# Softmax row sums without a stop in DRAM, and a plan that knows the DMA queue's limit, in a fused attention + mixer kernel

## The chip, the cores and the metric

The kernel runs on one core of a Trainium2 chip. TensorE (PE) multiplies matrices, ScalarE (ACT), VectorE (DVE) and GpSimd (POOL) do element-wise work, and SyncE (SP) issues nearly all DMAs, in the order in which they stand in its program. The metric is device time in microseconds (us) of one execution; lower is better.

## The reference

One token block of 2048 tokens x 512 features goes through two branches that share the input; a per-token gate mixes them.

```
g = sigmoid((x * gate_w).sum(-1))
a = attention(x)     # 32 heads of 16; q,k,v = x @ wqkv; softmax(q k^T / 4) v; then @ wo
h = gelu(layernorm(x) @ w1)          # four feature groups, shifted by +1,-1,+2,-2 tokens
x1 = x + shift(h) @ w2
b = x1 + gelu(layernorm(x1) @ w3) @ w4      # inner width 1792
out = g * a + (1 - g) * b
```

## The kernel before

**The work.** Attention scores are computed transposed, in tiles of 128 keys x 512 queries of one head: 2048 tiles in all. They come in 32 rounds of 64 tiles. A round is a chunk `c` of 512 queries, a group `G` of eight heads and a parity `p`, so it has four heads; four heads sit in the four 32-row groups of the PE array. A PE matmul (line L1536) puts one tile's scores into one of eight PSUM banks. Then the exponential is taken in one of two ways:

- ACT takes two or three banks in one `Exp` activation (L1631) and writes bf16 probabilities.
- DVE computes an approximation from the bits of the number (L1663), one bank at a time, and three shifted copies of a pair of tiles are made by DVE (L1706) and POOL (L1708); the four copies are added up by four PE matmuls instead of one.

The matmul with V (L1761) adds a tile into the round's accumulator bank. V has a column of ones, so row 0 of each head's 32-row group is the softmax row sum.

**The end of a round** (`finish_round`). DVE copies the accumulator to SBUF (`accsb`, L1782). The four row sums (4 x 512 floats) are spread over 128 partitions so that DVE can invert them quickly: one DMA stores them in DRAM (`den`, L1784), a second loads them as 128 x 16 (`pk`, L1786). DVE takes the reciprocal (L1789) and multiplies by the gate (L1790). A DMA stores the factors in DRAM (`rr`, L1792), four DMAs broadcast one row each to 32 partitions of `bcs` (L1796), POOL multiplies (`oT`, L1800), and four DMAs move each head's 16 rows to their place in `oD` (L1804), the operand of the output projection. `oD` of a pair of rounds (p = 0 and 1) belongs together. Other DMAs go through the same queue of SP: weights, the transposed loads of x (`DMA_TRANSPOSE`), and the layer norm's rows that POOL makes (`xn`, L1358), SP stores (`xn_dram`, L1362) and loads back transposed (L1368).

**The order.** Nothing is scheduled on the chip by itself: the kernel runs a model of the engines while it is built (`Sim`) and writes down instructions in the order in which the model started them. Each job has planned durations: `dma(lat, ..., hold)` is an SP job that holds the queue for `hold` ns and lands `lat` ns after its start. A table `STEPS` sets some 40 parameters of the planner's rules (priorities, how far ahead to work, how many tiles DVE may take) for each eighth of a round, 256 stages in all. On the chip every engine then runs its list in order, and waits where an operand is late. `start()` writes the first loads by hand with planned issue times, and `first()` writes the first transposes (L1206), projections (L1198) and copies by hand.

Of the kernel before, what the change touches and what calls it, by code (L numbers as in the profile page):

```python
# [11 lines left out]
ALU = mybir.AluOpType  # L12
BF16 = mybir.dt.bfloat16
F32 = mybir.dt.float32
# [177 lines left out]
class Sim:  # L192
# [6 lines left out]
    def __init__(self, slots):  # L199
# [24 lines left out]
        self.readers = {}  # L224
        self.usable = [0.0] * 8
# [108 lines left out]
    def try_engine(self, e):  # L334
# [136 lines left out]
def kernel(  # L471
# [77 lines left out]
        0: dict(P1_PRIO=0.312, GP2=0.15, DVE_STOP=8, DVE_STOP_L=12, DVE_ALONE=138, SL0=-150, SL1=130, IDLE_NS=864,  # L549
            BRES=2, AHEAD=16, PV_FULL=0.947, PV_IDLE=0.25, PRESS=22, ROT=1, AT_SH=118, HOLE=3, CAP3=5, LIMD=4, GATE=4,  # L550
            AFIRST=1, LIMA=2, JOIN=1),
        1: dict(P1_PRIO=0.743, S_PRIO=0.178, DVE_STOP_L=7, URG=2, DVE_ALONE=-158, SL0=45, SL1=0, PV_IDLE=0.731,
            E_PRIO=0.25, JOIN=2),
        2: dict(ROT=3, E_PRIO=2, ROWM=7),
        3: dict(P1_PRIO=0.414, S_PRIO=0.625, GP2=0.8, DVE_STOP_L=16, URG=3, DVE_ALONE=2, SL0=0, B_LOW=5, DVE_WAIT=2,
            AHEAD=24, AHEAD2=32, PV_IDLE=0.5, MAXU=3, DUE_SH=-6, AT_SH=69, MAXG=2, CAP3=0, LIMD=3, GATE=3, E_PRIO=0.25,
            AGE=6000, ROWM=3, JOIN=0),
        4: dict(GP2=1, EARLY=64, SL1=-150),
        5: dict(P1_PRIO=0.743, S_PRIO=0.3, DVE_STOP=2, DVE_STOP_L=7, URG_L=18, DVE_ALONE=362, SL1=60, B_LOW=8, BRES=4,
            AHEAD2=24, PV_FULL=0.916, PV_IDLE=0.25, PRESS=18, MAXU=2, ROT=2, HOLE=7, MAXG=1, CAP2=5, CAP3=7, AFIRST=2,  # L560
            AGE=9000, ROWM=99, LIMA=3),
        6: dict(P1_PRIO=0.312, S_PRIO=0.214, DVE_STOP=13, DVE_STOP_L=16, URG_L=12, DVE_ALONE=2, B_LOW=3, BRES=0,
            DVE_WAIT=1, AHEAD2=32, PV_FULL=1, PV_IDLE=0.117, ROT=0, DUE_SH=-14, HOLE=0, MAXG=3, GATE=4, AFIRST=1,
            AGE=3000, JOIN=1),
        7: dict(S_PRIO=0.38, E_PRIO=2, AGE=12000),
        8: dict(S_PRIO=0.214, DVE_STOP_L=7, URG=2, EARLY=99, IDLE_NS=537, B_LOW=0, BRES=4, AHEAD=3, AHEAD2=16,
            PV_IDLE=0.25, MAXU=4, ROT=2, DUE_SH=-6, E_PRIO=0.25, AFIRST=2, AGE=9000, LIMA=4, JOIN=0),
        9: dict(P1_PRIO=0.414, S_PRIO=0.3, DVE_STOP=6, DVE_STOP_L=16, URG=3, URG_L=18, DVE_ALONE=-81, SL0=130, SL1=130,
            IDLE_NS=459, B_LOW=5, BRES=2, DVE_WAIT=3, AHEAD=24, AHEAD2=32, PV_FULL=0.916, PV_IDLE=0.731, PRESS=22,
            MAXU=9, DUE_SH=-9, AT_SH=34, HOLE=3, MAXG=1, CAP2=6, CAP3=0, LIMD=4, GATE=3, E_PRIO=2, AGE=3000, LIMA=3,  # L570
            JOIN=1),
        10: dict(B_LOW=8, PRESS=26, MAXU=2, AFIRST=1, AGE=9000, ROWM=1),
        11: dict(AT_SH=69, ROWM=5),
        12: dict(S_PRIO=0.625, GP3=0.9, DVE_STOP=13, DVE_ALONE=-158, SL0=45, SL1=60, IDLE_NS=374, PV_FULL=0.86,
            PV_IDLE=0.25, MAXU=3, ROT=3, AT_SH=0, HOLE=2, CAP3=7, LIMD=3, AFIRST=2, AGE=20000, ROWM=0, JOIN=0),
        14: dict(MAXU=2),
        15: dict(DVE_WAIT=1, E_PRIO=0.1, AFIRST=1),
        16: dict(GP3=0.633, AHEAD2=24, HOLE=0, MAXG=3, LIMD=4, AFIRST=2, AGE=3000),
        17: dict(DVE_ALONE=362),
        18: dict(P1_PRIO=0.2, S_PRIO=0.5, GP2=0.3, GP3=0.967, DVE_STOP=8, URG_L=12, DVE_ALONE=-158, EARLY=64, SL0=130,  # L580
            SL1=45, DVE_WAIT=2, AHEAD=9, AHEAD2=32, PV_FULL=0.947, MAXU=7, ROT=2, AT_SH=34, HOLE=2, MAXG=1, CAP3=6,
            AFIRST=0),
        19: dict(MAXU=3),
        20: dict(DVE_WAIT=4, AHEAD=12, MAXG=2, AGE=6000),
        21: dict(CAP3=4, GATE=2, ROWM=1),
        22: dict(GP2=0.8, URG_L=18, DUE_SH=0),
        23: dict(GP2=0.15, DVE_WAIT=2, PV_IDLE=0.117),
        24: dict(P1_PRIO=0.136, S_PRIO=0.38, GP2=1, GP3=0.8, URG=11, DVE_ALONE=500, EARLY=99, SL0=0, SL1=0, IDLE_NS=864,
            B_LOW=0, BRES=0, DVE_WAIT=3, AHEAD=5, PV_FULL=0.97, MAXU=4, ROT=3, DUE_SH=32, HOLE=7, CAP3=0, GATE=3,
            E_PRIO=2, AFIRST=2, AGE=12000, ROWM=99, ACC2=2),  # L590
        25: dict(GP3=0.5, DVE_STOP=6, URG=2, DVE_ALONE=138, AHEAD=24, PV_IDLE=0.25, ROT=0, DUE_SH=-14, HOLE=2, CAP3=5,
            AGE=20000, ACC2=1),
        26: dict(GP2=0.15, URG=8, AHEAD=16, PV_FULL=0.813, CAP3=4, ACC2=2),
        27: dict(SL1=60, ACC2=1),
        28: dict(GP2=1, GP3=0.967, URG_L=12, DVE_ALONE=-81, SL1=0, PV_FULL=0.916, ACC2=2),
        29: dict(GP3=0.5, SL0=130, SL1=45, ROT=1, E_PRIO=0.1, LIMA=2),
        30: dict(DVE_STOP=2),
# [1578 lines left out]
```

## Time and profile before

| | |
|---|---|
| median of 3 runs | 731.88 us (731.85 to 732.23) |
| the profiled execution's own time | 731.34 us |
| its span, from first to last instruction | 729.4 us |
| ACT busy | 713.2 us (98%) |
| PE busy | 719.9 us (99%) |
| DVE busy | 698.0 us (96%) |
| POOL busy | 481.0 us (66%) |
| DMA | 38.27 MB in 69543 packets, mean 52 GB/s |

A matmul that was issued into a full pipeline counts as busy until its modelled end, so PE's share does not show whether PE had time to spare; the waits do. A group's "busy" is the union of its instructions in time, its mean is that of single instructions, which overlap at their ends. The profiled execution ran 0.54 us under the median of the timed runs.

### The profile page before, as it was taken

Reading aid. Unit: us, or ns where it says so; the run is one execution under the profiler, and the core shown is the slowest. Engines: PE = TensorE matmul, PEld = TensorE weight load, DVE = VectorE, ACT = ScalarE, POOL = GpSimd, SP = SyncE. Lnnn points to the kernel's source line nnn. Section 1 sums busy time; section 2 is a strip of 40 time slices with the busy share of each in tenths; the row PEclk is TensorE's granted clock in tenths of the full one; section 3 lists DMA queues with packets and bytes.
Section 4 is the critical chain, followed back from the end, with each engine's and each line's share of the span. In section 5 each row is a group of like instructions: output and inputs, shape, how many; then the busy total and the mean of one; then the engine's idle time right before and its main releaser. Section 6 shows DMA issues by size and latency. Waiting matters only on the chain.

```text
span 729.4 us, 23745 instructions
## 1 busy us (share of the span) xinstructions
PE 719.9 (99%) x9533; PEld 214.3 (29%) x9533; DVE 698.0 (96%) x1461; ACT 713.2 (98%) x728; POOL 481.0 (66%) x502
## 2 busy tenths in 40 slices
PE   9999999999999999999999999999999999999997
PEld 5334322232332222223222222222222232222222
DVE  6999899999999999999999999999999999999997
ACT  6999989999999999999999999999999999999995
POOL 2786767778786876685556556686777856564451
PEclk9999999999999999999999999999999999999999
DMA  9222422323123210141111101221100131000001
GB/s 188 79 61 54 101 71 46 65 50 89 61 67 79 59 41 22 45 137 53 24 26 35 28 22 29 63 80 28 41 19 21 36 102 26 25 28 21 18 19 40
DMA packets 69543, 38.27 MB, mean 52 GB/s; under 512 B 46893, under 2 KB 64317, under 8 KB 69433
## 3 DMA queue, kind: packets, MB, share of 16 engines
q1 hardware_dynamic: 68472, 36.23, 19.7%
q8 instruction: 74, 1.21, 0.7%
q10 hardware_dynamic: 960, 0.52, 0.3%
q14 instruction: 37, 0.29, 0.2%
HBM read 21.07 MB, written 6.81 MB: 38 GB/s over the span
## 4 chain that ended last, share of the span: by engine, by line
PE 80%; ACT 13%; DVE 2%; issue 2%; DMA 1%; POOL 1%; SPq 0%; ACTq 0%; DVEq 0%
PE banks L1761 29%; PE banks L1536 26%; PE banks L1134 24%; ACT prob L1631 12%; ACT hT L1378 1%; DVE prob L1706 1%; DMA wq<-in_A_wqkv_dram 1%; DMA xn_dram<-xn 1%; DVE prob L1663 0%; PE banks L2111 0%; POOL prob L1708 0%; ACT L1378 0%; DVE hB L1431 0%; PE banks L1291 0%; PE banks L1198 0%
## 5 line engine op out<-in xcount | busy, mean ns | idle before, releaser
L1631 ACT ACTIVATE prob<-banks 128x1024 bf16<-128x1024 f32 (+1 forms) x705 | 669.1, 1121 | 3.1 <-PE banks L1536 2.8
L1708 POOL TENSOR_SCALAR prob<-prob 128x1024 uint16<-128x1024 uint16 x364 | 374.5, 1047 | 180.7 <-DVE prob L1706 118.5
L1663 DVE TENSOR_SCALAR prob<-banks 128x512 uint16<-128x512 f32 (+1 forms) x577 | 385.0, 693 | 12.7 <-PE banks L1536 8.0
L1761 PE MATMUL banks<-prob,V 128*17 128x512 bf16 (+1 forms) x3818 | 319.6, 381 | 2.1 <-POOL prob L1708 1.5
L1536 PE MATMUL banks<-q,kT 32*128 32x512 bf16 x2048 | 275.7, 384 | 1.4 <-ACT prob L1631 0.2
L1706 DVE TENSOR_SCALAR prob<-prob 128x1024 uint16<-128x1024 uint16 x521 | 192.3, 423 | 3.6 <-POOL prob L1708 2.3
L1536 PEld LDWEIGHTS <-kT 32*128 32x128 bf16 x2048 | 69.1, 90 | 289.0 <-ACT prob L1631 265.5
L1761 PEld LDWEIGHTS <-V 128*17 128x17 bf16 (+1 forms) x3818 | 73.5, 88 | 120.0 <-issue 96.4
L1134 PE MATMUL banks<-xnT,w 128*32 128x512 bf16 x1152 | 92.1, 383 | 0.0
L1800 POOL TENSOR_TENSOR oT<-accsb,bcs 128x512 bf16<-128x512 f32 x31 | 39.5, 1275 | 28.8 <-DVE prob L1706 24.8
L1134 PE MATMUL banks<-w,hT 128*32 128x512 bf16 x696 | 57.6, 383 | 0.0
L1134 PEld LDWEIGHTS <-w 128*32 128x32 bf16 x1904 | 40.3, 95 | 48.3 <-issue 28.1
L1134 PE MATMUL banks<-w,w 128*32 128x256 bf16 (+1 forms) x752 | 38.0, 309 | 0.0
L1134 PE MATMUL banks<-w,hB 128*32 128x512 bf16 x448 | 37.7, 382 | 0.0
L1358 POOL TENSOR_SCALAR xn<-x_sb,rs,nm 128x512 bf16<-128x512 bf16 x32 | 25.0, 785 | 13.8 <-DVE prob L1706 3.7
L1145 PE MATMUL banks<-w,oD 32*128 32x512 bf16 x56 | 21.5, 384 | 0.0
L1338 DVE BATCH_NORM_STATS2 st<-x_sb 128x6 f32<-128x512 bf16 x32 | 21.4, 680 | 0.0
L1782 DVE COPY accsb<-banks 128x512 f32<-128x512 f32 x31 | 21.1, 680 | 0.1
L1134 PE MATMUL banks<-w,oD 128*32 128x512 bf16 x184 | 21.0, 384 | 0.1
L1134 PEld LDWEIGHTS <-hT 128*32 128x32 bf16 x696 | 14.9, 95 | 19.9 <-issue 14.0
L1134 PE MATMUL banks<-w,wq 128*32 128x512 bf16 x240 | 19.8, 383 | 0.0
L1378 ACT ACTIVATE hT<-hT 128x7168 bf16<-128x7168 bf16 (+1 forms) x3 | 19.4, 6452 | 0.0
(100 smaller groups left out, 273.6 us busy)
## 6 DMA issues: line engine op xcount, KB each, us to landing
bcs<-rr SPq DMA_DIRECT2D x124, 64.0 KB
xn_dram<-xn SPq DMA_DIRECT2D x32, 128.0 KB
w<-in_B_w_dram SPq DMA_DIRECT2D x8, 512.0 KB
w<-in_B_w_dram SPq DMA_DIRECT2D x8, 448.0 KB
oD<-oT SPq DMA_DIRECT2D x124, 16.0 KB
x_sb<-in_A_x_dram SPq DMA_DIRECT2D x3, 512.0 KB
out_dram<-ot SPq DMA_DIRECT2D x12, 128.0 KB
w<-in_A_wqkv_dram SPq DMA_DIRECT2D x2, 256.0 KB
```

The source lines that it names most:

```text
L1134: units.append([Op("col", j, lambda j=j, lf=lf, rf=rf, n0=n0, n1=n1, st=st, sp=sp: nc.tensor.matmul(get()[32 * j:32 * j + 32, n0:n1], lhsT ...
L1145: o = Op("row", i, lambda: nc.tensor.matmul(get(), lhsT=lf(0, P)[rows], rhs=rf()[rows], start=False, stop=True, tile_position=(32 * i, 0), ...
L1338: a = dve(600, deps, lambda: nc.vector.bn_stats(out=sb.slot[:], in_=x_sb[:, t, :]), prio=6, at=at, acq=[sb])
L1358: g = gp(750, [m], lambda t=t, xb=xb: nc.gpsimd.tensor_scalar(out=xb.slot[:], in0=x_sb[:, t, :], scalar1=rs[which][:, t:t + 1], scalar2=nm ...
L1378: g = nc.scalar.activation(out=ap, in_=ap, func=ACT.Gelu_apprx_tanh)
L1536: o = Op("row", i, lambda: nc.tensor.matmul(dst(), lhsT=kT[G][32 * i:32 * i + 32, kt * P:(kt + 1) * P], rhs=qbuf[G, c].slot[32 * i:32 * i ...
L1631: job = act(hold, ops, lambda: nc.scalar.activation(out=prob[:, pb.cut(), :].bitcast(BF16), in_=unit()[:, rb.cut(), :], func=ACT.Exp, scal ...
L1663: return nc.vector.tensor_scalar(out=prob[:, b0.cut() if w == 2 else b0.bufs[h0].slot, :], in0=unit()[:, rb.cut() if w == 2 else rb.bufs[0 ...
L1706: return nc.vector.tensor_scalar(out=cut(k), in0=cut(0), scalar1=float(SHIFT * k), scalar2=None, op0=ALU.add)
L1708: return nc.gpsimd.tensor_scalar(out=cut(k), in0=cut(0 if both else 2), scalar1=1.0, scalar2=float(SHIFT * (k if both else 1)), op0=ALU.mu ...
L1761: return nc.tensor.matmul(one(accs[r])[32 * i:32 * i + n, :], lhsT=lhs(n), rhs=rhs(), start=st and not edge, stop=True, tile_position=(0, ...
L1800: n = gp(1250, d3, lambda: nc.gpsimd.tensor_tensor(out=ob.slot[:], in0=ab.slot[:], in1=bb.slot[:], op=ALU.mult), acq=[ob], frees=[ab, bb], ...
```

## The change

In the order in which they act:

- **Start.** The load of the second chunk of x (512 KB) is made to wait for an earlier DMA, the third load of x rows; what stands behind it on SP waits with it. One of nine warm-up matmuls is dropped. Of the five copies of transposed x, ACT makes one and DVE four (before: two and three). The planned times of this piece are rewritten.
- **End of a round.** The row sums go from `accsb` to `pk` in one DMA within SBUF; `den` is gone. One DMA broadcasts all four rows of `rr`. For the first 30 rounds the whole of `oT` is stored in DRAM (`o_dram`) in one DMA, and once both rounds of a pair are there one DMA loads that pair's `oD`. Round 30 keeps the four direct DMAs; round 31 has none, as before.
- **Plan.** The model lets SP start a DMA only when the one eight places earlier has landed by its own reckoning (`sent`). Four small loads for the last chunk's gate (`zL`) are put off to tile 300 and later. The whole table `STEPS` has other values (245 entries, before 244), so the order of all engines is another one.

The 2048 tiles are split between the engines almost as before: ACT's program had 657 activations of two banks and 48 of three, and now has 661 and 45, which is one tile less for ACT and one more for DVE. In the rounds SP's program loses 31 `den` DMAs, 93 of 124 `bcs` and 120 of 124 `oD<-oT`, and gains 30 stores and 15 loads through `o_dram`: 199 DMAs less.

```diff
+        self.sent = [0.0] * 8
...
             end = max(end, self.queue + 1500.0)
+            land = max(self.t + 0.65 * (j.hold + j.lat), min(end, self.queue + 1500.0))
+            self.sent = self.sent[1:] + [land]
+            if self.sent[0] > self.t_free[e]:
+                self.t_free[e] = self.sent[0]
+                self.push(self.t_free[e], None)
...
     STEPS = {
-        0: dict(P1_PRIO=0.312, GP2=0.15, DVE_STOP=8, DVE_STOP_L=12, DVE_ALONE=138, SL0=-150, SL1=130, IDLE_NS=864,
+        0: dict(P1_PRIO=0.312, GP2=0.15, DVE_STOP=8, DVE_STOP_L=12, URG=8, DVE_ALONE=138, SL0=-75, SL1=130, IDLE_NS=864,
...
+    o_dram = dpool.tile([4 * NCH, 4, 2, 32, 512], BF16, name="o_dram")
...
+    def behind(inst, first):
+        tc.add_manual_dep(inst.ins, first.ins.name, mybir.DependencyInfo(
+            mybir.DependencyClass.Sync, mybir.DependencyReason.DATA), reason="load order")
...
-    j_x1 = [start("SP", 4900.0, lambda q: q.dma_start(out=x_sb[:, 4:8, :], in_=x_src(1, 0, 4)))]
+    issue["SP"] = 4500.0
+    j_x1 = [start("SP", 2900.0, lambda q: q.dma_start(out=x_sb[:, 4:8, :], in_=x_src(1, 0, 4)))]
+    behind(insts[-1], insts[2])
...
-        for _ in range(9):
+        for _ in range(8):
...
-                cp = nc.scalar.copy if i in (1, 3) else nc.vector.tensor_copy
+                cp = nc.scalar.copy if i == 2 else nc.vector.tensor_copy
...
-                in_=zE_dram[S - 512:S].rearrange("(b e) -> e b", e=32)), prio=6)
+                in_=zE_dram[S - 512:S].rearrange("(b e) -> e b", e=32)), prio=6).at = 300 + 20 * j
...
-            j_att[c].append(d)
+        for G in range(4 if c < NCH - 1 else 3):
+            j_att[c].append(dma(3300.0, [att_done[c * 8 + 2 * G], att_done[c * 8 + 2 * G + 1]], lambda c=c, G=G: nc.sync.dma_start(
+                out=oDbuf[c, G].slot[:], in_=o_dram[4 * c + G].rearrange("j p q n -> (j p) q n")[:, 1:DH + 1, :]),
+                acq=[oDbuf[c, G]], prio=1))
...
-        d0 = dma(2000.0, [e], lambda: nc.sync.dma_start(out=db.slot[:], in_=ab.slot[0:P:32, :]), prio=1, acq=[db],
-                 frees=[ab], hold=580.0)
-        d1 = dma(2800.0, [d0], lambda: nc.sync.dma_start(
-            out=kb.slot[:], in_=db.slot[:].rearrange("j (b e) -> (j b) e", e=16)), prio=1, acq=[kb], frees=[db],
-            hold=400.0)
+        d1 = dma(3000.0, [e], lambda: nc.sync.dma_start(out=kb.slot[:], in_=ab.slot[0:P:32, :]), prio=1, acq=[kb],
+                 frees=[ab], hold=450.0)
...
-        for j in range(4):
-            d3.append(dma(3000.0, [d2], lambda j=j: nc.sync.dma_start(
-                out=bb.slot[32 * j:32 * j + 32, :], in_=rb.slot[j, :].partition_broadcast(32)),
-                acq=[] if j else [bb], frees=[rb], prio=1))
-            d3[j].need = bb if j else None
...
+        d3 = dma(3400.0, [d2], lambda: nc.sync.dma_start(
+            out=bb.slot[:], in_=rb.slot[:].unsqueeze(1).broadcast_to([4, 32, 512])), acq=[bb], frees=[rb], prio=1)
...
+        if r < NR - 2:
+            dma(3200.0, [n], lambda: nc.sync.dma_start(out=o_dram[4 * c + G, :, p, :, :], in_=ob.slot[:]), frees=[ob, fin], prio=1,
+                hold=400.0)
+            return
```

Two places show how the order moves. The first is DVE at the very start, from the copies of the transposed first chunk (`w`) to the first query block (`q`); before:

```order
L1211 COPY w_97<-banks 128x2x256 x2
L1211 COPY w_97<-banks 128x256
L1216 CAST kT_64<-banks 128x256
L1218 TENSOR_SCALAR q_107<-banks,mE 128x256
L1224 TENSOR_SCALAR q_107<-banks,mO 128x256 x2
```

and now:

```order
L1224 COPY w_98<-banks 128x2x256 x2
L1224 COPY w_98<-banks 128x256 x2
L1229 CAST kT_64<-banks 128x256
L1231 TENSOR_SCALAR q_108<-banks,mE 128x256
L1237 TENSOR_SCALAR q_108<-banks,mO 128x256 x2
```

One more quarter-size copy stands on DVE, and the sequence behind it is the same.

The second is SP from the first broadcast of a round's factors to the row sums of round 2. `bcs`, `rr`, `oT`, `oD`, `den` and `pk` are the buffers of the round's end told above, `xnT` is the transposed load of the normalised x, `w<-in_B_w` a weight load; before:

```order
L1796 DMA bcs_113<-rr_134 32x512 x4
L1368 DMA_TRANSPOSE xnT_104<-xn_dram 128x512 x4
L1796 DMA bcs_113<-rr_135 32x512 x4
L1804 DMA oD_116<-oT_114 16x512 x4
L1082 DMA w_102<-in_B_w_dram 128x4x512
L1362 DMA xn_dram<-xn_105 128x512
L1362 DMA xn_dram<-xn_106 128x512
L1804 DMA oD_116<-oT_115 16x512 x4
L1784 DMA den_133<-accsb_111 4x512
L1362 DMA xn_dram<-xn_105 128x512
L1786 DMA pk_130<-den_133 128x16
```

and now:

```order
L1381 DMA_TRANSPOSE xnT_105<-xn_dram 128x512 x2
L1807 DMA bcs_114<-rr_132 128x1x512
L1375 DMA xn_dram<-xn_106 128x512
L1375 DMA xn_dram<-xn_107 128x512
L1807 DMA bcs_114<-rr_133 128x1x512
L1813 DMA o_dram<-oT_115 4x32x512
L1095 DMA w_103<-in_B_w_dram 128x4x512
L1375 DMA xn_dram<-xn_106 128x512
L1375 DMA xn_dram<-xn_107 128x512
L1800 DMA pk_131<-accsb_112 128x1x16
```

From the first broadcast to the landing of round 2's row sums SP issued 26 DMAs, and now issues 9. Four transposed loads stood between the two rounds' broadcasts; two of them now stand ahead of the first broadcast and two ahead of those shown.

More of the change, by code (lines that the diff above doesn't have):

```diff
@@ L973 @@
         "pk": slots("pk", 3, [P, 16], F32),
-        "den": slots("den", 3, [4, 512], F32, dpool),
         "rr": slots("rr", 3, [4, 512], F32, dpool),
@@ L1228, in first @@
         sim.emit(t, mm)
[L1229 to L1231 removed]
+        sim.t_free["PE"], sim.arr, sim.mode = t + 3440.0, [t + 3520.0] * 4, "full"
+        sim.push(t + 3440.0, None)
+        at_time(t + 2200.0, bt[1:])
         for k in range(KT):
[L1233 to L1236 removed]
+            j_xT[0, 0, k] = at_time(t + 2200.0)
+        j_q[0, 0, 0] = at_time(t + 3550.0)
+        j_ka.append(at_time(t + 3070.0, [ba, wb["x00"], wb["x00"], wb["k"]]))
+        j_k[0, 0] = act(275, [at_time(t + 3520.0)], lambda: nc.scalar.copy(out=kT[0][:, 256:512], in_=one(bb)[:, 0:256]),
                         prio=0, frees=[bb])
@@ L1452, in mlp2_down @@
                     lambda G=G: W("o")[:, G, :]) for G in range(ng)]
-            wdeps = [dl_w["o"]] + j_att[c][:2 * ng]
+            wdeps = [dl_w["o"]] + j_att[c][:ng]
             last = c == NCH - 1
@@ L1833 @@
             PLAN["w4", 4 * c + t] = int(a + (b - a) * t / 4)
-    first(3450.0)
+    first(3480.0)
     begun = [j_ka[0], j_q[0, 0, 0]]
```

730 lines of the change are left out of this document (360 added, 370 removed).

## The prediction

> **What bounds the kernel now.** I read the page's busy times first, then ACT's groups by shape, then the waits, then the timeline where ACT starts, stops and stalls.
>
> ```profile
> PE 719.9 (99%) x9533; PEld 214.3 (29%) x9533; DVE 698.0 (96%) x1461; ACT 713.2 (98%) x728; POOL 481.0 (66%) x502
> L1631 ACT ACTIVATE prob<-banks 128x1024 bf16<-128x1024 f32 (+1 forms) x705 | 669.1, 1121 | 3.1 <-PE banks L1536 2.8
> ...
> L1631 ACT ACTIVATE prob<-banks 128x1024 bf16<-128x1024 f32 x657 | 614.0, 1089 | 2.9 <-PE banks L1536 2.7
> L1631 ACT ACTIVATE prob<-banks 128x1536 bf16<-128x1536 f32 x48 | 74.0, 1550 | 0.2 <-PE banks L1536 0.2
> ...
> PEld L1536 <- ACT prob L1631: 265.5, 640, 0.6
> ```
>
> Three engines look full. The wait row decides: the score matmuls' weight loads waited 640 times, 265.5 us in all, for ACT to give banks back, while ACT's exponentials sat idle 3.1 us for anything. So ACT is the bound and PE follows it. The three places where ACT does not stream are its start, its end and one stretch between:
>
> ```profile
> 8.78 5.97 ACT L1631 ACTIVATE prob<-banks 128x1536 bf16<-128x1536 f32 x5 [0.17 <-PE banks L1536]
> ...
> 333.35 11.99 ACT L1631 ACTIVATE prob<-banks 128x1024 bf16<-128x1024 f32 x13
> ...
> 713.07 7.47 ACT L1631 ACTIVATE prob<-banks 128x1024 bf16<-128x1024 f32 x8
> ...
> 721.50 0.72 DVE L2122 STREAM_TRANSPOSE accsb<-banks 128x512 f32<-128x512 f32 x1 [1.60 <-PE banks L1761]
> ```
>
> The first exponential starts at 8.78, the last ends at 713.07 + 7.47 = 720.54, and the tail to 729.4 is 8.9 us. A quiet stretch has 13 two-bank exponentials in 11.99 us; the last takes some 1.09 to its end (the mean of one in the row of 657), so one comes every (11.99 - 1.09) / 12 = 0.908 us. By the same 0.18 us of overlap a three-bank one takes 1.550 - 0.18 = 1.37. Then the 705 need 657 x 0.908 + 48 x 1.37 = 662.3 us, and they held ACT for 669.1 + 3.1 = 672.2. So between start and tail at most 9.9 us can be had without taking work off ACT.
>
> **The start.** The chain of waits and the timeline:
>
> ```profile
> 1.68 4.56 DMA wq<-in_A_wqkv_dram
> ```
> ```profile
> 1.12 3.06 PE L1113 MATMUL banks<-zero 128*128 128x384 bf16 x9 [1.12 <-DVE zero L1102]
> ...
> 2.17 0.58 SPq L1053 DMA_DIRECT2D x_sb<-in_A_x_dram  x1
> ...
> 3.97 1.91 PE L1206 MATMUL banks<-idb,x_sb 128*128 128x128 bf16 x16
> ...
> 5.07 1.01 ACT L1211 COPY w<-banks 128x512 bf16<-128x512 bf16 x2 [1.44 <-PE banks L1206]
> ...
> 6.28 0.61 PE L1198 MATMUL banks<-w,wq 128*128 128x256 bf16 x4 [0.39 <-DMA wq<-in_A_wqkv_dram]
> ...
> 9.13 1.07 PE L1165 MATMUL banks<-idb,x_sb 128*128 128x128 bf16 x16
> ```
>
> The first projection waited for `wq`, on its way for 4.56 us, while the 512 KB of the second chunk, issued at 2.17, shared the DMA engines. The transposes were done at 3.97 + 1.91 = 5.88. Holding the big load takes that wait: -0.39 us. A warm-up matmul is a ninth of 3.06 us, so dropping one lets the transposes start up to 0.34 earlier, if x is there; the copies that the first projection needs then end on DVE instead of on ACT, and no later. Together -0.73. Against it: the transposes took 1.91 us for 16, and the same 16 at 9.13 took 1.07, so the array was still slow until about 5.6, and projections that begin sooner may run slow. Four at 6.28 took 0.61; at half speed they take some 0.4 more. The range is 0 to -0.8, and I take **-0.7**, as only the first projections can still fall into the slow time. What the hold costs: SP itself stands until x rows are there, about when the transposes begin (3.97), so the second chunk (2.17 before), the V weights and eight transposed loads behind them are issued about 2 us later. The transposes at 9.13 cover that if the load then lands in about 4 us from its issue; if it is 0.6 late, ACT's third exponential is, and the gain sinks to the lower end.
>
> The Trainium skill's page "TensorE: Matmul & The Clock Gate", in Part 1, says that the array runs at half speed until about 3.4 us of sustained work have been seen. By that rule alone the array, at work from 1.12, would have been fast from some 4.5 us on, and the start would gain the full 0.73 (an estimate by that page); the two transpose rows put the change later, and the measurement decides.
>
> **The stretch from 72 to 100 us.** The groups of that window, then what SP, POOL, DVE and ACT did in it:
>
> ```profile
> L1631 ACT ACTIVATE prob<-banks 128x1024 bf16<-128x1024 f32 (+1 forms) x28 | 26.9, 1101 | 2.4 <-PE banks L1536 2.4
> ```
> ```profile
> 69.41 1.72 SPq L1796 DMA_DIRECT2D bcs<-rr  x4
> 76.97 2.58 SPq L1796 DMA_DIRECT2D bcs<-rr  x4
> 79.59 3.13 SPq L1804 DMA_DIRECT2D oD<-oT  x4
> 84.47 2.41 SPq L1804 DMA_DIRECT2D oD<-oT  x4
> 86.98 0.54 SPq L1784 DMA_DIRECT2D den<-accsb  x1
> ```
> ```profile
> 72.83 1.28 POOL L1800 TENSOR_TENSOR oT<-accsb,bcs 128x512 bf16<-128x512 f32 x1 [1.69 <-DMA bcs<-rr]
> 82.20 1.27 POOL L1800 TENSOR_TENSOR oT<-accsb,bcs 128x512 bf16<-128x512 f32 x1 [2.37 <-DMA bcs<-rr]
> 87.66 2.02 POOL L1358 TENSOR_SCALAR xn<-x_sb,rs,nm 128x512 bf16<-128x512 bf16 x2 [1.15 <-DMA xn_dram<-xn]
> ```
> ```profile
> 90.73 0.43 DVE L1706 TENSOR_SCALAR prob<-prob 128x1024 uint16<-128x1024 uint16 x1 [2.29 <-POOL prob L1708]
> 91.97 0.25 DVE L1789 RECIPROCAL pk<-pk 128x16 f32<-128x16 f32 x1 [0.81 <-DMA pk<-den]
> ```
> ```profile
> 92.36 1.02 ACT L1631 ACTIVATE prob<-banks 128x1024 bf16<-128x1024 f32 x1 [1.14 <-PE banks L1536]
> 94.27 1.02 ACT L1631 ACTIVATE prob<-banks 128x1024 bf16<-128x1024 f32 x1 [0.89 <-PE banks L1536]
> 95.67 2.99 ACT L1631 ACTIVATE prob<-banks 128x1024 bf16<-128x1024 f32 x3 [0.37 <-PE banks L1536]
> ```
>
> This is one causal chain. SP was issuing broadcasts and head moves without a break from 76.97 to 86.88, and three stores and loads behind them came late. POOL stood 1.69 + 2.37 + 1.15 = 5.2 us for DMAs, DVE 2.29 for POOL and 0.81 for the row sums, and ACT lost 1.14 + 0.89 + 0.37 = 2.4 us for scores that PE could not issue. The price is a little more, since the overlap is lost too: from 92.36 to 94.27 and to 95.67 are steps of 1.91 and 1.40, and the one before 92.36 began some 1.02 + 1.14 earlier; three steps took 5.47 us instead of 3 x 0.908, which is 2.75 more. It is nearly all of the idle time that ACT's exponentials show for scores (2.4 of 2.8 us in the run). The new SP order has 9 DMAs in that place instead of 26, and the plan now counts the queue's depth, so it no longer puts POOL's and DVE's work where its data can't be. The ends are 0 (the jam moves elsewhere) and -2.8 (all of it goes); I take **-2.8**, since three separate causes in the chain, the four broadcasts, the head moves and the `den` hop, shrink at once.
>
> **The quiet rounds.** The round's DMAs late in the run:
>
> ```profile
> 698.48 2.43 SPq L1804 DMA_DIRECT2D oD<-oT  x4
> 701.80 0.53 SPq L1784 DMA_DIRECT2D den<-accsb  x1
> 703.50 0.34 SPq L1786 DMA_DIRECT2D pk<-den  x1
> ...
> 709.04 1.72 SPq L1796 DMA_DIRECT2D bcs<-rr  x4
> 715.55 2.42 SPq L1804 DMA_DIRECT2D oD<-oT  x4
> ```
> ```profile
> 704.93 1.21 PE L1134 MATMUL banks<-w,oD 128*32 128x512 bf16 x12
> ```
>
> Per round SP's issue time falls by the `den` DMA's 0.53, three quarters of 1.72 and most of 2.42, some 3.5 us; a hop of 703.50 - 701.80 = 1.7 us goes, and a store plus a load take the place of the direct moves, one landing more, bounded by that same hop: 1.7 to 3 us. None of it is on ACT's path: `oD` of the last pair but one was issued at 698.48 and first used at 704.93, and the other pairs have hundreds of microseconds. So **0**, and at most 1 us late at 704.93, where PE would stand with two or three banks of scores issued ahead.
>
> **ACT's own work.** Four two-bank exponentials more and three three-bank ones less: 4 x 0.908 - 3 x 1.37 = **-0.5**. The tail code is the same: 0.
>
> **The sum.** -0.7 - 2.8 - 0.5 = -4.0 on a profiled time of 731.34: 727.3. The median lies 0.54 above the profiled execution (731.88), so I forecast **727.9**. The rest of the new table reorders everything but takes nothing else off ACT; I cost it at 0, with the 9.9 us above as the bound of a gain, and the rivals below for a loss.
>
> **The rivals.**
>
> *The small gaps go too.* A plan that knows the queue may also lift part of the other 9.9 - 2.8 = 7.1 us of short stalls. Half of them gives 727.9 - 3.5 = 724.4, all of them 720.8. For it: all 256 stages are set anew. Against it: those gaps come from PE and banks and not from DMAs, as DVE's waits for DMAs are the 0.8 us above and POOL's are the rows above. 0.22.
>
> *The jam only moves.* Two rounds' ends pile up there because the gate's result comes late, and that is unchanged. If the stall comes back a little later in the same size, what is left is -0.5 and a start gain of 0.3: 731.1. 0.09.
>
> *The one broadcast is slow* (the other side). Its destination is 128 partitions, but its source has four rows, and one DMA of 4 x 64 KB could run on four of the 16 DMA engines.
>
> ```profile
> q1 hardware_dynamic: 68472, 36.23, 19.7%
> ...
> bcs<-rr SPq DMA_DIRECT2D x124, 64.0 KB
> ```
>
> 36.23 MB took 19.7% of 16 x 729.4 engine-us, 63 engine-us per MB, so 256 KB take 16.6: 1.0 us on 16 engines, 4.2 on four. Before, `bcs` landed 72.83 - 69.41 = 3.4 us after the first of four issues, 2.0 after the last; the plan now counts 3.4 in all. On four engines the landing comes at 2.0 - 1.0 + 4.2 = 5.2, 1.8 us behind the plan, in each of 31 rounds. In the jam 5.2 us of POOL's waits cost ACT 2.4, about 0.46 for one. If every round's lateness met a POOL that was ready, 31 x 1.8 x 0.46 = 26 us would be lost; the plan's slack decides, and from 9 us of POOL waits on (a sixth of that) the gain of 4.0 is used up. With a third of it the time is 727.9 + 8.6 = 736.5. Against it: only the two `oT` of the jam waited for `bcs` at all, the other 29 came after its landing anyway (in the last round 715.55, where the moves begin, less 1.28 is 5.2 us after 709.04), and 63 engine-us per MB is an average over small packets, while these are 2 KB each. 0.12.
>
> The Trainium skill's page "DMA: Bandwidth & Descriptors", in "Why a DMA increments its semaphore by 16 and not by 1", says that the number of engines is the largest up to 16 that divides the outermost sizes of both sides. For 4 and 128 that is four, which speaks against this edit; the former pieces, 32 rows each, got 16. No run here shows it yet.
>
> **How the numbers follow.** The forecast has 0.57: 725.5 to 730.4. About 0.2% (1.5 us) is what a measurement of this kernel can tell from no change, so "same" is 730.4 to 733.3. Faster: 0.57 + 0.22 = 0.79; same: the moved jam, 0.09; slower: 0.12. The range reaches down to 722.5, between half and all of the small gaps, and up to 732.5, over the moved jam and a slow broadcast that just eats the gain.
>
> **What would show it.** Right: the first exponential at 8.0 or sooner and no `wq` wait over 0.2; no idle of ACT over 0.5 between 72 and 100; SP never at work for 10 us without a break there; POOL's waits for `bcs` still few. Wrong: the second chunk's transposes waiting for x at 8 to 9 us; DVE's reciprocal waiting for the row sums; POOL waiting for `bcs` in round after round and PE behind it; a stall of ACT of over 2 us at another place.

## The result, and the profile after

The changed kernel took **736.73 us** at the median (736.26 to 737.13, four runs), the kernel before 731.87 (731.83 to 732.23, four runs on the same chip): a ratio of 1.0065, with a 95% interval of 1.0048 to 1.0082. It is slower by 4.9 us. The forecast was 727.9, faster by 4.0, with a range up to 732.5; the sign was wrong and the time lies outside. The third rival, *the one broadcast is slow*, had been worked out at 736.5. Two runs of the experiments below, at 917.1 and 834.8 us with granted clocks of 0.66 and 0.75, lay far outside all others and are left out of every figure.

The busy times, the exponentials and POOL's product with the factors on the page of the changed kernel (the code has moved by some lines: 1631 is now 1647, 1706 is 1722, 1800 is 1809):

```profile
span 734.7 us, 23442 instructions
PE 721.3 (98%) x9558; PEld 216.3 (29%) x9559; DVE 708.2 (96%) x1456; ACT 715.7 (97%) x728; POOL 487.3 (66%) x507
L1647 ACT ACTIVATE prob<-banks 128x1024 bf16<-128x1024 f32 (+1 forms) x706 | 671.9, 1099 | 6.2 <-PE banks L1552 4.6
L1809 POOL TENSOR_TENSOR oT<-accsb,bcs 128x512 bf16<-128x512 f32 x31 | 41.0, 1324 | 34.5 <-DMA bcs<-rr 19.2
bcs<-rr SPq DMA_DIRECT2D x31, 256.0 KB
```

The exponentials' own idle has doubled, from 3.1 to 6.2 us, and 4.6 of that is for scores. DVE is busy for 10.2 us more (708.2 against 698.0) with five instructions fewer. And POOL's product stood idle for 34.5 us before its 31 instances, 19.2 of them for the broadcast (before: 28.8 us, 4.1 of them for the broadcast). POOL's row in the waits of the changed kernel (us in total, times, longest):

```profile
POOL oT L1809 <- DMA bcs<-rr: 19.2, 14, 4.3
```

Before there were two such waits, the 1.69 and 2.37 of the jam that the prediction quotes. Now there are 14 among 31 rounds. The chain of waits of the changed kernel (start, us, what) has the broadcast on it as well, early and late:

```profile
1.68 4.09 DMA wq<-in_A_wqkv_dram
70.57 5.67 DMA bcs<-rr
79.42 7.60 DMA xn_dram<-xn
...
603.26 4.95 DMA bcs<-rr
```

The start came as forecast in direction, with the first exponential at 8.32 instead of 8.78. The first projections still stood 0.24 us for `wq`, and the second chunk's transposes (8.66) did not wait for their held load. The timeline of the changed kernel (start, us, engine, line, the idle before in brackets):

```profile
5.81 0.61 PE L1211 MATMUL banks<-w,wq 128*128 128x256 bf16 x4 [0.24 <-DMA wq<-in_A_wqkv_dram]
8.66 1.07 PE L1178 MATMUL banks<-idb,x_sb 128*128 128x128 bf16 x16
8.32 5.97 ACT L1647 ACTIVATE prob<-banks 128x1536 bf16<-128x1536 f32 x5 [0.17 <-PE banks L1552]
```

The jam did not go. In the timeline of the changed kernel it stands at 82 to 91 us, SP's issues first, then POOL, then ACT:

```profile
70.57 0.58 SPq L1807 DMA_DIRECT2D bcs<-rr  x1
77.62 0.55 SPq L1807 DMA_DIRECT2D bcs<-rr  x1
76.31 1.28 POOL L1809 TENSOR_TENSOR oT<-accsb,bcs 128x512 bf16<-128x512 f32 x1 [1.59 <-DMA bcs<-rr]
84.53 1.27 POOL L1809 TENSOR_TENSOR oT<-accsb,bcs 128x512 bf16<-128x512 f32 x1 [4.26 <-DMA bcs<-rr]
87.18 1.52 POOL L1371 TENSOR_SCALAR xn<-x_sb,rs,nm 128x512 bf16<-128x512 bf16 x2 [1.38 <-DMA xn_dram<-xn]
81.79 5.83 ACT L1647 ACTIVATE prob<-banks 128x1024 bf16<-128x1024 f32 x6 [0.77 <-PE banks L1552]
87.84 1.02 ACT L1647 ACTIVATE prob<-banks 128x1024 bf16<-128x1024 f32 x1 [0.22 <-PE banks L1552]
90.76 5.61 ACT L1647 ACTIVATE prob<-banks 128x1024 bf16<-128x1024 f32 x6 [1.90 <-PE banks L1552]
```

ACT's group for the stretch from 72 to 100 us, which the prediction shows for the kernel before (28 exponentials, 2.4 us idle), is now:

```profile
L1647 ACT ACTIVATE prob<-banks 128x1024 bf16<-128x1024 f32 x28 | 26.3, 1077 | 3.0 <-PE banks L1552 2.9
```

SP's issue time did shrink as forecast (0.58 for a broadcast instead of 1.72 or 2.58), but POOL waited for broadcasts as before, 1.59 and 4.26 us, and ACT lost 0.77 + 0.22 + 1.90 = 2.89 us. These two products began 76.31 - 70.57 = 5.74 and 84.53 - 77.62 = 6.91 us after the issue of their broadcast, where the plan has 3.4. ACT's loss over the whole run can be counted from the starts of all the exponentials: a two-bank one takes 0.904 us to the next start where nothing stalls, a three-bank one 1.331. With that and ACT's other work taken off, ACT stalled for 19.7 us between its first and last exponential, against 13.4 before: 6.3 more. With 0.46 gained at the start, 0.4 at ACT's own work and 0.2 in the tail that makes 5.2; the profiled executions differ by 734.7 - 729.4 = 5.3.

How long one broadcast takes shows in the DMA view of each kernel from the issue of the last round's broadcast on (each figure is the rate over 0.12 us); first the kernel after:

```profile
GB/s 0 0 0 0 0 0 0 0 0 0 0 51 51 51 51 34 119 85 119 85 119 85 119 85 102 102 102 102 102 102 102 102 102 51 51 188 34 17 0 0
```

Nothing moves for 1.3 us, and then 256 KB move at about 100 GB/s; the packets of 2 KB ran from 715.38 to 718.60, 3.22 us, so the data was there 4.6 us after the issue at 714.05 and POOL's product began after 5.04. In no round of this kernel did the product begin sooner than 4.86 us after the broadcast's issue. The plan counts 3.4. A stretch within another round's broadcast, in the table by stretches (us, busy and instructions of PE, PEld, DVE, ACT and POOL, granted clock, DMA share, GB/s):

```profile
699.20:702.00 2.80, 2.80 (x39) 0.77 (x35) 2.69 (x6) 2.80 (x4) 2.40 (x3) 1.00 0.23 91
```

A DMA share of 0.23 is 3.7 of 16 engines, so I read it as the broadcast from four rows running on four. This agrees with the rule that the prediction cites from the Trainium skill's page "DMA: Bandwidth & Descriptors", section "Why a DMA increments its semaphore by 16 and not by 1".

### The profile page after: what moved, and what is told of

It is laid out like the page before. It is cut to its first block, busy times and chain, and to the rows that moved or that the text cites. A ratio compares the mean times of both kernels' runs of the same rounds, so it can differ in the third digit from the quotient of the medians.

```text
span 734.7 us, 23442 instructions
## 1 busy us (share of the span) xinstructions
PE 721.3 (98%) x9558; PEld 216.3 (29%) x9559; DVE 708.2 (96%) x1456; ACT 715.7 (97%) x728; POOL 487.3 (66%) x507
## 4 chain that ended last, share of the span: by engine, by line
PE 80%; ACT 7%; DVE 6%; DMA 3%; issue 2%; POOL 1%; SPq 0%; DVEq 0%; POOLq 0%; ACTq 0%
PE banks L1777 29%; PE banks L1552 27%; PE banks L1147 23%; ACT prob L1647 5%; DVE prob L1722 3%; DVE prob L1679 2%; DMA bcs<-rr 1%; DMA xn_dram<-xn 1%; ACT hB L1391 1%; POOL prob L1724 1%; DMA wq<-in_A_wqkv_dram 1%; PE banks L2120 0%; POOL xn L1371 0%; PE banks L2098 0%; DVE accsb L1798 0%
## 5 line engine op out<-in xcount | busy, mean ns | idle before, releaser
L1724 POOL TENSOR_SCALAR prob<-prob 128x1024 uint16<-128x1024 uint16 x369 | 378.7, 1046 | 171.6 <-DVE prob L1722 113.1
L1722 DVE TENSOR_SCALAR prob<-prob 128x1024 uint16<-128x1024 uint16 x519 | 201.1, 443 | 1.4 <-PE banks L1777 0.9
L1777 PEld LDWEIGHTS <-V 128*17 128x17 bf16 (+1 forms) x3821 | 75.1, 88 | 121.3 <-issue 94.8
L1809 POOL TENSOR_TENSOR oT<-accsb,bcs 128x512 bf16<-128x512 f32 x31 | 41.0, 1324 | 34.5 <-DMA bcs<-rr 19.2
L1147 PE MATMUL banks<-w,hT 128*32 128x512 bf16 x692 | 62.0, 383 | 0.2 <-DVE accsb L1798 0.2
L1444 DVE CAST hB<-banks 128x512 bf16<-128x512 f32 x28 | 18.8, 675 | 0.2 <-PE banks L1147 0.2
```

The lines of the kernel that those rows point to most:

```text
L1147: units.append([Op("col", j, lambda j=j, lf=lf, rf=rf, n0=n0, n1=n1, st=st, sp=sp: nc.tensor.matmul(get()[32 * j:32 * j + 32, n0:n1], lhsT ...
L1722: return nc.vector.tensor_scalar(out=cut(k), in0=cut(0), scalar1=float(SHIFT * k), scalar2=None, op0=ALU.add)
L1724: return nc.gpsimd.tensor_scalar(out=cut(k), in0=cut(0 if both else 2), scalar1=1.0, scalar2=float(SHIFT * (k if both else 1)), op0=ALU.mu ...
L1777: return nc.tensor.matmul(one(accs[r])[32 * i:32 * i + n, :], lhsT=lhs(n), rhs=rhs(), start=st and not edge, stop=True, tile_position=(0, ...
L1809: n = gp(1250, [d3], lambda: nc.gpsimd.tensor_tensor(out=ob.slot[:], in0=ab.slot[:], in1=bb.slot[:], op=ALU.mult), acq=[ob], frees=[ab, bb ...
```

## The experiments

The theory after this result (A): the landing of the one broadcast, 1.2 us behind the plan by its data and some 1.5 by the product's start, costs the kernel what the rest of the change gains. Rivals: the new order itself is worse (B), or the row sums' or heads' new path is (C). Ratios are against the kernel before, run beside each experiment on the same chip; its medians there were 731.95 to 732.39.

### Four broadcasts in the place of the one

Everything is as in the changed kernel, its order too; only the broadcast is four DMAs again.

```diff
-        d3 = dma(3400.0, [d2], lambda: nc.sync.dma_start(
-            out=bb.slot[:], in_=rb.slot[:].unsqueeze(1).broadcast_to([4, 32, 512])), acq=[bb], ...
+        d3 = dma(3400.0, [d2], lambda: [nc.sync.dma_start(
+            out=bb.slot[32 * j:32 * j + 32, :], in_=rb.slot[j, :].partition_broadcast(32)) for j in range(4)][-1],
```

> The changed kernel with every engine's order as it is, but the broadcast of a round's factors is issued as four DMAs of 32 partitions each, one behind the other at the place of the one. Theory A (the one broadcast lands about 5.0 us after its issue, since few DMA engines carry it, where the plan counts 3.4): oT follows 3.4 to 4.5 us after the first issue, POOL's waits for bcs fall from 19.2 us to under 5, ACT's losses between exponentials fall by 4 to 7 us, time 730 to 732.5. Theory B (the new order itself stalls ACT, whatever the broadcast does): POOL's waits fall too, but the time stays at 735 to 737.5.

Measured: **727.9 us** (727.56 to 728.59, six runs), ratio 0.9946 (0.9928 to 0.9964). That is 8.8 us below the changed kernel, and the forecast's own number; it is also below the 730 that theory A had allowed, so the late landing cost more than expected. The span, the groups of the page, and POOL's wait in this kernel:

```profile
span 725.6 us, 23598 instructions
L1647 ACT ACTIVATE prob<-banks 128x1024 bf16<-128x1024 f32 (+1 forms) x706 | 668.4, 1113 | 1.2 <-PE banks L1552 0.7 <-POOL prob L1724 0.4
POOL oT L1810 <- DMA bcs<-rr: 1.3, 1, 1.3
```
```profile
L1647 ACT ACTIVATE prob<-banks 128x1024 bf16<-128x1024 f32 x31 | 28.7, 1105 | 0.4 <-POOL prob L1724 0.4
```

The exponentials' idle is 1.2 us instead of 6.2, POOL waits once for `bcs`, and in the stretch from 72 to 100 us (the second fence, its groups) there are 31 exponentials with 0.4 us idle, where the kernel before had 28 with 2.4 and the changed kernel 28 with 3.0. The last round's broadcast in this kernel's DMA view, from its first issue:

```profile
GB/s 0 0 0 0 0 0 0 34 85 85 171 120 273 137 154 103 137 137 137 154 154 205 69 34 0 0 0 0 0 0 0 0 0 0 0 0 137 68 0 0
```

The first of the four starts while SP is still issuing the others, and the data is there 2.9 us after the first issue instead of 4.6. Theory A is borne out, and B and C fall as causes of the loss: the new order and the other edits are all in this kernel.

### The one broadcast in the kernel before

```diff
-            d3.append(dma(3000.0, [d2], lambda j=j: nc.sync.dma_start(
-                out=bb.slot[32 * j:32 * j + 32, :], in_=rb.slot[j, :].partition_broadcast(32)),
+            d3.append(dma(3000.0, [d2], lambda j=j: None if j else nc.sync.dma_start(
+                out=bb.slot[:], in_=rb.slot[:].unsqueeze(1).broadcast_to([4, 32, 512])),
```

> The kernel before with every engine's order as it is, but its four broadcast DMAs are one, at the place of the first. Theory A: the landing moves from 3.4 to about 5.0 us after the first issue; in the former order oT stood 4.2 to 5.9 us after it, so only some rounds wait: POOL's waits for bcs grow from 4.1 to 8 to 16 us and the time rises by 1 to 4 us, to 733 to 736. Theory B: the broadcast is harmless, time 731.3 to 732.5.

Measured: 733.43 us (731.79 to 735.25, ten runs), ratio 1.0016 (1.0001 to 1.0031): some 1.2 us slower, not 8.8. POOL's wait:

```profile
POOL oT L1800 <- DMA bcs<-rr: 7.8, 7, 3.6
```

Seven waits and 7.8 us, where the kernel before has two and 4.1, cost 1.2. In the old order most products stood late enough for the slow landing: set against each round's first issue in the trace before, 6 of the 31 began sooner than 4.86 us, the earliest in the changed kernel with its one broadcast. In the new order, with four broadcasts, 12 did. So the price of the slow broadcast depends on the order around it, and the slack that the prediction read off the old order was not there in the new one.

### The planned landing set to what the trace shows

```diff
-        d3 = dma(3400.0, [d2], lambda: nc.sync.dma_start(
+        d3 = dma(5100.0, [d2], lambda: nc.sync.dma_start(
```

> The changed kernel with one number of the plan changed: the one broadcast is planned to land after 5100 ns instead of 3400, so the planner makes another order with the same table of parameters. Theory A: POOL's waits for bcs fall under 6 us and the time falls, though the table was not made for this plan: 731 to 735. Theory B: it stays between 735 and 738, or gets worse, since the table fits the order less.

Measured: 782.19 us (781.84 to 783.56), ratio 1.069 (1.0659 to 1.0722): a miss by 47 us. The two largest waits of ACT in this kernel, and what POOL still waits for the broadcast:

```profile
ACT prob L1647 <- PE banks L1552: 27.8, 24, 5.8
ACT w L2148 <- PE banks L2120: 9.9, 2, 9.7
POOL oT L1809 <- DMA bcs<-rr: 6.0, 4, 3.3
```

POOL waits for `bcs` less than in the changed kernel (6.0 us against 19.2), and ACT stands far longer all the same. The planner had re-made the whole order with the new number, and, as I read it, the hand-set table of the stages no longer fitted. To separate the number from the order, the next kernel changes it by as little as 100 ns, in the fast four-broadcast version.

```diff
-        d3 = dma(3400.0, [d2], lambda: [nc.sync.dma_start(
+        d3 = dma(3500.0, [d2], lambda: [nc.sync.dma_start(
```

> Four broadcast DMAs, planned to land after 3500 ns instead of 3400: a harmless number (they land after 3.4 us), but the planner makes another order with a table that was set for the old one. If a true plan is what counts, the time stays at 727 to 730. If the table fits only the plan that it was made for, it rises by 5 us or more, and e4_true_plan's 782 says nothing about 5100 ns.

Measured: **769.4 us** (769.25 to 770.07), ratio 1.0518 (1.0497 to 1.0539), 41 us above the same kernel with 3400. The transfers are the same; only the order differs. The waits:

```profile
ACT prob L1647 <- PE banks L1552: 16.8, 17, 6.7
POOL oT L1810 <- DMA bcs<-rr: 10.8, 5, 5.0
```

Even the quick broadcast is waited for in five rounds of this order, yet that is 10.8 us of a loss of 41. Neither of these two runs can price the landing, since both change the order with it. They show that a planned time cannot be mended in this kernel without setting the table anew.

### The hold of the second chunk's load

Left out of the changed kernel, and then of the four-broadcast version:

```diff
-    behind(insts[-1], insts[2])
```

> The changed kernel without the dependency that holds the second chunk's load; the orders stay. If the hold is what brought the first exponential from 8.78 to 8.32 us, it comes at 8.6 to 8.9 again and the time rises by 0.3 to 0.6, to 737.0 to 737.4. If the dropped warm-up matmul and the moved copies did it, nothing changes: 736.5 to 737.0.

> Four broadcast DMAs in the changed order (as before in e1_four_bcs, 727.9) and no hold on the second chunk's load. If the hold is worth what the first exponential shows: it comes at 8.6 to 8.9 instead of 8.1 to 8.3 and the time is 728.3 to 728.9. If the hold is worth nothing: 727.5 to 728.2.

Measured: 735.82 us (735.11 to 738.43, eight runs) without it in the changed kernel, which says nothing: the difference to 736.73 on another chip is within the spread, and it has the wrong sign for a hold that helps, although the first exponential of the profiled run came later, at 8.91 us. In the four-broadcast version 729.19 (727.68 to 730.26, twelve runs), a little above what was expected, against 727.9 and 728.23 with the hold, on other chips. That would make the hold worth 1.0 to 1.3 us, but the intervals of the ratios still touch (0.9949 to 0.9971 without it; 0.9928 to 0.9964 and 0.9928 to 0.9955 with it), and the changed kernel does not confirm it. In the slowest of these runs, the profiled one, the weight loads of the first projection waited, and the projections behind them ran slowly:

```profile
PEld L1210 <- DMA wq<-in_A_wqkv_dram: 1.0, 1, 1.0
```
```profile
6.35 1.03 PE L1210 MATMUL banks<-w,wq 128*128 128x256 bf16 x4 [0.79 <-DMA wq<-in_A_wqkv_dram]
7.18 1.06 PE L1210 MATMUL banks<-w,w 128*128 128x256 bf16 x4
```

Four projections took 1.03 to 1.06 us here, against 0.60 in the changed kernel, and the first exponential came at 10.32 us. Over all profiled executions, the first projections stood 0.39 to 1.20 us for `wq` in the four without the hold, and at most 0.53 in the ten with it, where seven show no such idle of PE. So that wait differs from run to run, and with the hold it is mostly gone. The spread of the times does not show it: the kernel before, without the hold, ran from 729.4 to 734.5 on these chips, but the changed kernel, with it, from 734.4 to 737.0 in its repeat below.

### The changed kernel again, and the row sums by way of DRAM

The changed kernel on another chip:

> The changed kernel itself, beside the next three on one chip. Theory A and B both: 735.5 to 737.5. With 256 KB of broadcast on four DMA engines, the stretch of a late round's broadcast shows a DMA share of about 0.25; POOL waits 15 to 23 us for bcs.

Measured: 736.87 us (734.36 to 737.03), ratio 1.0061 (1.0042 to 1.008); POOL's waits for `bcs` in its profile are 12.5 us in 12, fewer than the 15 to 23 expected. The loss is the kernel's, not a chip's, and it does not follow POOL's waits one to one.

The four-broadcast version with the old hop of the row sums through `den`, the plan unchanged:

```diff
+        def hop(den=sim.free["den"][r % 3]):
+            nc.sync.dma_start(out=den[:], in_=ab.slot[0:P:32, :])
+            return nc.sync.dma_start(out=kb.slot[:], in_=den[:].rearrange("j (b e) -> (j b) e", e=16))
-        d1 = dma(3000.0, [e], lambda: nc.sync.dma_start(out=kb.slot[:], in_=ab.slot[0:P:32, :]), ...
+        d1 = dma(3000.0, [e], hop, prio=1, acq=[kb], frees=[ab], hold=450.0)
```

> Four broadcast DMAs in the changed order, and the row sums go by way of DRAM again (den, then pk, in the place of the one copy; the plan counts 3000 ns for both). The hop adds about 1.7 us in each of 31 rounds. Theory A in its general form (a landing later than planned is paid, since the order has the consumer at the planned time): DVE's reciprocal waits 0.5 to 1.5 us in most rounds, 15 to 40 us in all, and the time is 733 to 745. If the order has slack there, DVE waits under 5 us and the time stays under 730.

Measured: 739.76 us (739.11 to 741.76), ratio 1.0116 (1.0096 to 1.0136), 11.9 us above the four-broadcast version:

```profile
DVE pk L1805 <- DMA pk<-den: 12.2, 13, 2.1
```

DVE waits 12.2 us in 13 rounds, less than the 15 to 40 expected, and about as much is lost. It fits theory A on another wait: a landing later than the plan's number is paid by the engine that stands in an order set to that number. A part of it can be the further issue on SP in each round; the last experiment below bears on that.

### A broadcast from sixteen rows

If four engines are the cause, one DMA from sixteen rows should be quick. The factors are stored four times over (by four small stores), and one DMA broadcasts them:

```diff
+        d2 = dma(2300.0, [r2], lambda: [nc.sync.dma_start(
+            out=rb.slot[j].rearrange("r (b e) -> b r e", e=16),
+            in_=kb.slot[32 * j:32 * j + 32, :].unsqueeze(1).broadcast_to([32, 4, 16])) for j in range(4)][-1], ...
+        d3 = dma(3400.0, [d2], lambda: nc.sync.dma_start(
+            out=bb.slot[:], in_=rb.slot[:].rearrange("j r n -> (j r) n").unsqueeze(1).broadcast_to([16, 8, 512])), ...
```

> One broadcast DMA again, in the changed order, but its source is 16 rows: the factors are stored four times over (four small stores of 32 partitions in the place of the one), so that the outer sizes are 16 and 128. If few source rows confine a DMA to few engines, this one runs on 16: its packets take under 1.2 us instead of 3, POOL's waits for bcs are under 5 us, and the time is 727.5 to 730, as with four broadcast DMAs. If one DMA of 256 KB is slow as such, it stays at 735 to 738.

Measured: 734.79 us (733.86 to 736.96), ratio 1.004 (1.0026 to 1.0053): the time was missed. A stretch in the table by stretches that is just the broadcast's packets, SP's issues ahead of it, and POOL's wait:

```profile
701.99:703.22 1.23, 1.23 (x22) 0.39 (x23) 0.90 (x2) 1.23 (x2) 0.32 (x1) 1.00 0.58 212
```
```profile
695.96 1.73 SPq L1805 DMA_DIRECT2D rr<-pk  x4
700.64 0.56 SPq L1809 DMA_DIRECT2D bcs<-rr  x1
```
```profile
POOL oT L1812 <- DMA bcs<-rr: 10.9, 9, 3.4
```

The packets took 1.23 us instead of 3.22, at twice the rate, so the row count is what sets how quick one broadcast of these bytes is. But from the first store of the factors to the broadcast's issue passed 700.64 - 695.96 = 4.7 us in this round, where the changed kernel's last round needs 714.05 - 712.59 = 1.46. This round is one of the longer ones; at the median of the 31 rounds it is 3.2 us against 1.5. The lateness moved one DMA ahead, and POOL still waited 10.9 us.

### Half the bytes

The other way to shorten it: one DMA from four rows as in the changed kernel, with the factors stored in bfloat16 (they are rounded to that), 128 KB instead of 256.

```diff
-        "rr": slots("rr", 3, [4, 512], F32, dpool),
+        "rr": slots("rr", 3, [4, 512], BF16, dpool),
...
+        d3 = dma(3400.0, [d2], lambda: nc.sync.dma_start(
+            out=bb.slot[:].bitcast(BF16)[:, 0:512], in_=rb.slot[:].unsqueeze(1).broadcast_to([4, 32, 512])), ...
```

> One broadcast DMA from four rows, as in the changed kernel and in its order, but the factors are bf16: 128 KB instead of 256 (the product keeps its bf16 output; the factors are rounded). On four engines the packets take half as long, about 1.5 us instead of 3, and the landing comes 3.4 to 3.6 us after the issue, where the plan has it. Theory A (the price is the landing against the plan): POOL's waits for bcs under 5 us, time 726.5 to 729. If one DMA in the place of four is bad for another reason (its issue, its rows), it stays at 734 to 738.

Beside it, the four-broadcast version on the same chip:

> The four broadcast DMAs in the changed order once more, beside the kernel with bf16 factors on one chip: 727.5 to 728.6. If SP's issue time counts at the places where its queue is dense, it is 0.5 to 1.5 us slower than h1_half_bytes, which issues 93 DMAs less.

Measured: **727.17 us** (726.58 to 727.21, five runs), ratio 0.993 (0.9918 to 0.9943), the quickest of all; the four broadcasts 728.23 (727.41 to 728.38), ratio 0.9941 (0.9928 to 0.9955). The last round's broadcast from its issue on in the DMA view, the product's group on the page, and ACT's timeline in the place of the jam:

```profile
GB/s 0 0 0 0 0 0 0 0 0 0 0 26 68 94 85 94 94 102 102 102 85 94 85 51 9 0 0 0 0 0 0 0 0 0 0 0 137 0 0 0
```
```profile
L1809 POOL TENSOR_TENSOR oT<-accsb,bcs 128x512 bf16<-128x512 f32 x31 | 35.9, 1160 | 18.3 <-DVE prob L1722 10.8 <-PE banks L1552 3.6 <-PE banks L1777 2.7
```
```profile
65.25 31.43 ACT L1647 ACTIVATE prob<-banks 128x1024 bf16<-128x1024 f32 x34
```

The rate is again about 100 GB/s, which fits four engines again, but the data is there 3.0 us after the issue, ahead of the planned 3.4. No `bcs` is left among what POOL waits for, and ACT streams through the jam, 34 exponentials in one run of 31.43 us. The broadcast in one DMA is not bad by itself; its landing time was. One thing more differs in this kernel: POOL's product with bfloat16 factors takes 1.16 us instead of 1.28. That may be a part of the 1.1 us by which it beats the four broadcasts, beside the issues that it saves; the two were not separated.

### Every head row stored twice

Does SP's and the store's time matter in the new order? The four-broadcast version, each `oT` stored a second time to a place that nothing reads:

```diff
-            dma(3200.0, [n], lambda: nc.sync.dma_start(out=o_dram[4 * c + G, :, p, :, :], in_=ob.slot[:]), ...
+            dma(3200.0, [n], lambda: [nc.sync.dma_start(out=t[4 * c + G, :, p, :, :], in_=ob.slot[:]) for t in (o2_dram, o_dram)][-1], ...
```

> Four broadcast DMAs in the changed order, and each round's oT is stored twice, into two places, the place that is read last. This doubles the cost of the store on SP and delays the loads behind it. If the way of the heads' rows through DRAM is off the path, as the prediction had it at 0, the time is 727.5 to 728.8. If SP's time or the landing of oD is on it: 730 to 735.

Measured: 732.90 us (732.47 to 734.59), ratio 1.0015 (1.0001 to 1.0028): 5.0 us more, where off the path it should have cost nothing.

```profile
DVE pk L1803 <- DMA pk<-accsb: 4.1, 4, 1.7
POOL xn L1372 <- DMA xn_dram<-xn: 2.6, 1, 2.6
ACT prob L1648 <- PE banks L1553: 4.6, 5, 1.9
```

The waits name DMAs that stand behind the extra stores on SP, and ACT loses its scores at three places, before 89.55, 114.27 and 137.82 us (1.88, 0.74 and 1.35 us). So an extra store is on the path in the dense places of SP's queue. Whether by its half microsecond of issue or by the 128 KB that it moves was not separated.

## Why the prediction was wrong

**The step that failed** is in "The quiet rounds": the broadcast went into the sum as SP issue time saved and nothing else ("three quarters of 1.72"), at a cost of 0, while its landing stood only in a rival with a chance of 0.12. That term measured +8.8 us (736.73 with the one broadcast, 727.9 with four in its place; 736.87 and 728.23 in the repeats). The rival's mechanism was the right one: a landing in 5.2 us, where the product began about 5.0 after the issue and the data was there after 4.6; engines 4 of 16, where the share was 0.23. That its 736.5 us lies so near the measured 736.73 is in part luck: the "third" of 26 us, 8.6, was chosen without a reason.

**Why it got 0.12.** The argument against it was that 29 of 31 products came after the landing anyway. Of those 29 it gave one, the last round's, 5.2 us after the issue; that a product did not wait for a landing at 3.4 us does not say that it had slack up to 5.2. In the trace before, 6 of the 31 products began within 4.86 us, so even there the slack was not in every round, though one broadcast in that order cost only 1.2 us. And the change brought a new order, made with 3.4 us for the landing, in which 12 began that early once the broadcasts were quick, and in the changed kernel 14 waited. The slack of the old order was no evidence on the new one; the planned number and the estimate beside it (5.2 against 3.4) were, and they stood in the prediction.

**What was right.** With the broadcast's landing mended, the median came out at the sum's own number, 727.9 (728.23 in the repeat). That the match is so close is in part luck, since the terms did not all come out at their size:
- the start at -0.7: the four-broadcast kernel's first exponential is at 8.08 in one profiled execution and 8.42 in its repeat (8.78 before), the changed kernel's at 8.32 and 8.66. So the start gave -0.1 to -0.7. In the repeat at 8.42 the first four projections took 1.02 us instead of 0.61, the 0.4 more that the prediction had named against this term; and in the execution at 8.08 the second chunk's transposes waited 0.51 us for their held load, which it had named as a sign of being wrong;
- the jam at -2.8: 31 exponentials instead of 28 between 72 and 100 us, idle 0.4 instead of 2.4 (30 and 0.7 in the repeat). Over the whole run ACT's stalls fell by 2.3 us, to 11.1 (11.4 in the repeat). In the changed kernel it came back at 82 to 91, since POOL's first link, the wait for `bcs`, was still there. Of the "three separate causes" that were to shrink at once, one did not shrink;
- ACT's own work at -0.5: -0.4, from the measured 0.904 and 1.331 us of one exponential;
- the tail at 0: 8.4 us instead of 8.9 behind the last exponential, a gain of 0.4 that the sum did not have.

**What was right in the number but not in the reason.** The store and load through DRAM were booked at 0 because the heads are used late. As built they cost nothing that shows, though no run put the direct moves of the heads back. But "None of it is on ACT's path" left SP out: a second store cost 5.0 us, and the row sums' hop, booked as hidden too, cost 11.9 when put back under the same plan. In the dense places of this order an extra DMA on SP is paid. The edits were free as built, and I read that as the plan's doing, since it counts their times; that their results are used late was not the reason.

**What stays open** is how the 8.8 us split. POOL waited 19.2 us for the broadcasts; DVE became slower too. Its shift of the probabilities, in the groups by shape of the changed kernel and of the four-broadcast kernel:

```profile
L1722 DVE TENSOR_SCALAR prob<-prob 128x1024 uint16<-128x1024 uint16 x516 | 200.5, 444 | 1.4 <-PE banks L1777 0.9
```
```profile
L1722 DVE TENSOR_SCALAR prob<-prob 128x1024 uint16<-128x1024 uint16 x516 | 191.4, 427 | 0.9 <-PE banks L1777 0.5
```

That is 9.1 us of DVE time for the same 516 instructions. By place, about 2.7 us of the loss lie between 72 and 100 us (three exponentials fewer); the rest is in short stalls over the whole run. Whether ACT lost its scores to POOL's late product or to DVE's longer shifts was not separated; both go away with the late landing.

## What to carry to other kernels

Count a merged DMA by its landing and not by the issues it saves: look at how many rows it reads from, and so on how many engines it can run, and put that time beside the one that the consumer's place in the order assumes. Where a change brings a new order, slack seen in the old trace is no evidence; the new order's own numbers are. And where such a transfer is late, cutting its bytes can do what splitting does, with fewer issues.

## What the runs showed of the hardware

- A broadcast of 256 KB took 3.22 us of packets from four source rows (715.38 to 718.60) and 1.23 us from sixteen; half the bytes from four rows took 1.6 us (706.37 to 707.97). The first packets came 1.33 to 1.35 us after the issue in these three.
- Four small stores that write 64-byte pieces four times over let the broadcast behind them go 3.2 us after the first issue (median of 31 rounds; 4.7 in the round shown), where one plain store let it go after 1.5. Most of that is SP's issue time, 1.73 us for the four against 0.32 for the one.
- Some of DVE's shifts are slow while POOL works. Instances that overlap POOL's work in time took 452 ns in the mean before and 546 in the changed kernel, the others 417 and 416. Half of the overlapping ones are not slowed (median 418), and a tenth of them took 890 ns and more in the changed kernel. There 111 overlap, 20 of them mainly the late product, at 697 ns in the mean; with four broadcasts 88 overlap, at 477. That makes up the 9 us of DVE time, and no row of the waits shows it.
